# Attention sums in 42 PSUM columns per head, a bf16 state update, and GpSimd left with the mask: a mixed attention and feed-forward kernel

## The chip, the cores and the metric

One NeuronCore of one Trainium2 chip runs the whole program. The metric is the device time of one execution in microseconds (us). The engines are TensorE (PE; its weight loads are listed as PEld), VectorE (DVE), ScalarE (ACT), GpSimd (POOL) and the DMA queue that SyncE issues (SP, in waits SPq). Each engine takes its instructions in the order in which they stand in its program, so an instruction that waits holds up those behind it.

## The reference, cut to what matters

Gated linear attention over 4 batches, 8 heads, 768 steps, head size 40, and then two feed-forward layers over the 3072 tokens (320 to 2048 to 320).

```python
for t in range(S):
    m_new = np.maximum(f_gate[:, :, t] + m, i_gate[:, :, t])
    f_stab, i_stab = np.exp(f_gate[:, :, t] + m - m_new), np.exp(i_gate[:, :, t] - m_new)
    C = f_stab * C + i_stab * outer(v_t, k_t)      # 40 x 40 state per head
    n = f_stab * n + i_stab * k_t
    y[:, :, t] = sigmoid(o_t) * (C @ q_t) / np.maximum(np.abs(n @ q_t), 1.0)
h = np.maximum(x @ w1_in, 0.0);  x = h * h @ w1_out
h = x @ w2_in;  out = h * sigmoid(h) @ w2_out
```

Everything is float32.

## The kernel before, in words

**Attention** runs in 24 tiles of 128 steps of one batch (`TILES`: two batches alternate, six chunks each). In a tile the products within the chunk are matmuls, and a state per batch (`cc2`, 40 rows by 42 columns per head: 40 values, the sum n, a zero) carries over what came before. Tiles 0 to 5 (`N_NAT`) use plain float32 matmuls, the 18 others split float32 numbers into pieces that TensorE multiplies faster. The steps of a tile are functions: `load_a` and `load_b` (DMA of q, k, v; of the broadcast gates `W` and `eq`), `SK`/`SK2` (split q and k on ACT and DVE, then nine small DMAs that restack them, L282 and L284), `WT` (causal mask on POOL L290, exponentials on ACT L294), `SC` (scores, L309, and on DVE their split into three bf16 pieces p1, p2, p3, L316 to L323), `VK` (pieces of v and k, mostly POOL), `QT` (scaled q), `HG` (per head the products p times v and q times state, L400 to L415), `EV` (division and output gate, DVE L426 to L438), `ST` (state update, L476 to L494), `XT` (transpose of the result, L500, to the input x of the feed-forward layers).

In `HG` a head owns 84 PSUM columns, two halves of 42: one matmul of a p piece streams two pieces of v side by side, so four matmuls per head do, and a head group needs two PSUM tiles, hA and hB. `EV` then adds the halves with two TENSOR_REDUCE (L426). `ST` does the same with float32r pieces: six matmuls (khi and klo against vs), two PSUM tiles, two reduces (L478). All these tiles, the scores and the transposes share one PSUM pool of three buffers (tag `at`): seven of them go by per tile of attention.

**Feed-forward layer 1** runs beside attention in 8 blocks of 384 tokens, 16 steps j each: `emit_in` (eight matmuls into `hin`, L569; ACT takes Relu L576 and Square L577; for even j ACT squares again, L579, for odd j DVE does, L581 (`G_PAT = "ad"`); DVE then forms `gl`, L588) and `emit_out` (eight matmuls into `o`). Layer 2 follows alone, 8 blocks more, and is not touched.

**What sets the order.** TensorE's order is written by hand: a table `plan(i)` gives each function of tile i a due time in steps j, relative to `base(i)`; tiles stand 16/3 steps apart. On the other engines a scheduler orders the instructions by its own estimate. During blocks 1 to 6, every sixth step loads one of layer 2's 16 weight pieces, decodes it on ACT, DVE and POOL (`w_split`, L169 to L200) and stores it (L202), all called at one step.

Two small tables choose engines: `ENG` sends `vr`, `vlo`, `kw`, `klo`, `qt`, `ql`, `um`, `clo` and the low parts of weights to POOL.

Of the kernel before, what the change touches and what calls it, by code (L numbers as in the profile page):

```python
# [31 lines left out]
N_NAT = 6  # L32
# [5 lines left out]
G_PAT = "ad"  # L38
# [21 lines left out]
def mlstm_moe_kernel(  # L60
# [104 lines left out]
    def w_split(raw, which, layer, u, pl):  # L165
# [7 lines left out]
        if which == "i":  # L173
# [8 lines left out]
            on("lo_i").tensor_tensor(out=w[:, 3:5], in0=tv[:, 0:2], in1=f(w[:, 0:2]), op=ALU.subtract)  # L182
            on("lo_r").tensor_tensor(out=w[64:128, 2], in0=tv[64:128, 2], in1=f(w[64:128, 2]), op=ALU.subtract)
        else:
# [15 lines left out]
            on("lo_o").tensor_tensor(out=ol, in0=tv, in1=f(oh), op=ALU.subtract)  # L200
        if layer == 2:
            sp.dma_start(out=w2_d[which, u], in_=f(ws))  # L202
# [47 lines left out]
    def load_b(i):  # L250
# [4 lines left out]
        sp.dma_start(out=w, in_=g_d[b * H:(b + 1) * H, c * L:(c + 1) * L].unsqueeze(0).to_broadcast([128, H, L]))  # L255
        if c % EC == 0 and c + EC > 1:
            for g in range(3):
# [3 lines left out]
                             in_=e_d[h:h + n, c * L:(c + EC) * L].unsqueeze(1).to_broadcast([n, 40, EC * L]))  # L261

# [62 lines left out]
    def VK(i):  # L325
# [31 lines left out]
    def QT(i):  # L357
# [6 lines left out]
        on("qt", i).tensor_tensor(out=q, in0=q, in1=eqv(i)[0:120], op=ALU.mult)  # L364
# [3 lines left out]
        on("ql", i).tensor_tensor(out=ql[0:120], in0=q, in1=f(qh[0:120]), op=ALU.subtract)  # L368

    def HG(i, g):  # L370
# [20 lines left out]
        if g == 2:  # L391
            d["hB"] = p_at.tile([128, 512], F32, tag="at", name="hB")
        ps = d["hA"] if g < 2 else d["hB"]
        ov = ps[:, 0:504].rearrange("p (h a c) -> p h a c", a=2, c=42)
        o0 = 3 * (g % 2)
        st = True
        if c:
            k = 40 * n
            cs = cs2[b % 2][0:k, 3 * g:3 * g + n]
            pe.matmul(ov[:, o0:o0 + n], d["qh"][0:k, g], cs, start=True, stop=False)  # L400
            pe.matmul(ov[:, o0:o0 + n, 0], d["ql"][0:k, g], cs[:, :, 0], start=False, stop=False)
            st = False
        for x in (range(n) if HORD else range(n - 1, -1, -1)):
            h = 3 * g + x
            p1, p2, p3 = (d[p, h // 4][:, (h % 4) * L:(h % 4 + 1) * L] for p in ("p1", "p2", "p3"))
            v12, v3 = d["v12"][:, h], d["v3"][:, h]
            o = ov[:, o0 + x]
            if st:
                pe.matmul(o, p2, v12, start=True, stop=False)
                pe.matmul(o[:, 0], p3, v12[:, 0], start=False, stop=False)  # L410
            else:
                pe.matmul(o[:, 0], p3, v12[:, 0], start=False, stop=False)
                pe.matmul(o, p2, v12, start=False, stop=False)
            pe.matmul(o[:, 1], p1, v3, start=False, stop=False)
            pe.matmul(o, p1, v12, start=False, stop=st or x == (n - 1 if HORD else 0))  # L415

    def EV(i):
        d = T[i]
        den = at.tile([128, H, 1], F32, tag="den", name="den")
        if i < N_NAT:  # L420
            hn = d["hA"][:, 0:VW].rearrange("p (h c) -> p h c", c=42)
            act.activation(out=den, in_=hn[:, :, 40:41], func=ACTF.Abs)
        else:
            hn = at.tile([128, H, 42], F32, tag="hn", name="hn")
            for ps, h0, n in ((d["hA"], 0, 6), (d["hB"], 6, 2)):
# [411 lines left out]
```

## Time and profile before

| | |
|---|---|
| median of 3 runs | 932.18 us (930.99 to 933.9) |
| the profiled execution: own time, span | 925.65 us, 923.9 us |
| TensorE busy, granted clock over the span | 844.3 us (91%), 0.987 |
| DVE, ACT, POOL busy | 572.0 us (62%), 497.6 us (54%), 255.8 us (28%) |

The span has two parts. Up to about 578 us attention and layer 1 run together, and every engine works; behind it layer 2 runs alone on a TensorE that is busy in every slice. "Busy" of TensorE is an upper bound, since matmuls overlap in the pipe and their ends are modelled; starts of successive matmuls tell the real rate.

### The profile page before, as it was taken

What the parts mean: (1) busy time and instruction counts of PE and PEld (TensorE: products, weight loads), DVE (VectorE), ACT (ScalarE), POOL (GpSimd) and SP (SyncE); (2) the same over time, 40 slices, a digit from 0 to 9 for tenths busy, and PEclk for the clock granted to TensorE, in tenths of its full rate; (3) what the DMA queues carried; (4) which work ended last, traced back from release to release, by engine and by line L of the source; (5) the groups of instructions that cost most, each with busy time, mean ns of one, the idle gap of its engine ahead of it and who ended that gap; (6) DMA issues with size and microseconds to landing.
All of it is one profiled execution on the core that took longest, in us unless ns stands there. A gap on an engine that the chain in (4) does not pass through costs nothing.

```text
span 923.9 us, 14980 instructions
## 1 busy us (share of the span) xinstructions
PE 844.3 (91%) x5460; PEld 821.4 (89%) x5460; DVE 572.0 (62%) x953; ACT 497.6 (54%) x1061; POOL 255.8 (28%) x271
## 2 busy tenths in 40 slices
PE   3868979889898988988899999999999999999998
PEld 3758969789788988887788999999999999999998
DVE  5567557976888987987987534444445444444343
ACT  3677556665676766665664555343434343444343
POOL 6675344642344555555522010000000000000000
PEclk9999999999999998999999999999999999999999
DMA  8793345555756546545634387110101010000000
GB/s 245 243 299 126 123 150 161 191 153 176 250 176 220 163 140 226 192 140 195 224 123 147 107 309 239 49 57 1 56 1 56 1 57 1 23 1 22 1 22 22
DMA packets 72579, 117.45 MB, mean 127 GB/s; under 512 B 5306, under 2 KB 54394, under 8 KB 72266
## 3 DMA queue, kind: packets, MB, share of 16 engines
q1 hardware_dynamic: 72506, 116.50, 39.1%
q8 instruction: 43, 0.70, 0.3%
q14 instruction: 30, 0.25, 0.1%
HBM read 77.23 MB, written 19.33 MB: 105 GB/s over the span
## 4 chain that ended last, share of the span: by engine, by line
PE 55%; DMA 13%; DVE 12%; ACT 8%; SPq 6%; issue 3%; POOL 2%; ACTq 0%; POOLq 0%; DVEq 0%
PE hin L569 27%; PE o L621 6%; PE o L619 6%; PE o L620 6%; SPq L284 3%; DMA vk<-in_vk_dram 3%; ACT W L294 2%; DMA eq<-e_d 2%; DMA stk<-tt 2%; DMA raw<-in_w_in_dram 2%; PE o L602 2%; DVE gl L588 2%; PE o L603 2%; PE o L604 2%; SPq L282 1%
## 5 line engine op out<-in xcount | busy, mean ns | idle before, releaser
L569 PE MATMUL hin<-x,wi 128*128 128x384 f32 x2048 | 416.7, 345 | 23.6 <-ACT r L576 10.5
L569 PEld LDWEIGHTS hin<-x,wi 128*128 128x128 f32 x2048 | 364.6, 192 | 29.7 <-ACT r L576 12.9
L588 DVE TENSOR_TENSOR gl<-r,gh 128x384 fp32r<-128x384 f32 x256 | 163.6, 642 | 92.0 <-ACT gh L585 68.2
L584 DVE TENSOR_TENSOR r<-hin,r 128x384 f32<-128x384 f32 x128 | 71.3, 557 | 122.1 <-ACT r L583 122.1
L583 ACT ACTIVATE r<-hin 128x384 f32<-128x384 f32 x128 | 63.0, 492 | 132.4 <-PE hin L569 132.4
L621 PE MATMUL o<-wo,gl 128*128 128x320 f32 x384 | 118.7, 309 | 0.0
L619 PE MATMUL o<-wo,gh 128*128 128x320 f32 x384 | 118.3, 308 | 0.0
L620 PE MATMUL o<-wo,gh 128*128 128x320 f32 x384 | 117.8, 307 | 0.0
L585 ACT ACTIVATE gh<-r 128x384 fp32r<-128x384 f32 x128 | 67.2, 525 | 74.0 <-DVE r L584 74.0
L602 PE MATMUL o<-gh,wo 128*128 128x384 f32 x256 | 90.5, 353 | 4.3 <-ACT ob L612 3.8
L576 ACT ACTIVATE r<-hin 128x384 f32<-128x384 f32 x128 | 61.4, 480 | 57.8 <-PE hin L569 39.2
L604 PE MATMUL o<-gl,wo 128*128 128x384 f32 x256 | 86.8, 339 | 1.4 <-DVE gl L588 1.4
L603 PE MATMUL o<-gh,wo 128*128 128x384 f32 x256 | 86.8, 339 | 0.0
L619 PEld LDWEIGHTS o<-wo,gh 128*128 128x128 f32 x384 | 72.1, 188 | 0.0
L620 PEld LDWEIGHTS o<-wo,gh 128*128 128x128 f32 x384 | 72.1, 188 | 0.0
L621 PEld LDWEIGHTS o<-wo,gl 128*128 128x128 f32 x384 | 72.0, 187 | 0.0
L647 POOL TENSOR_TENSOR xr<-xr 128x384 f32<-128x384 f32 x8 | 8.1, 1017 | 230.0 <-DMA xr<-x_d 179.7
L294 ACT ACTIVATE W<-W,aw 128x128 f32<-128x128 f32 x192 | 60.2, 389 | 17.0 <-POOL W L290 16.9
L577 ACT ACTIVATE gh<-r 128x384 fp32r<-128x384 f32 x128 | 66.5, 521 | 2.2
L581 DVE TENSOR_TENSOR r<-r 128x384 f32<-128x384 f32 x64 | 47.1, 737 | 21.5 <-ACT gh L577 21.5
L602 PEld LDWEIGHTS o<-gh,wo 128*128 128x128 f32 x256 | 49.0, 191 | 5.6 <-ACT ob L612 4.5
L604 PEld LDWEIGHTS o<-gl,wo 128*128 128x128 f32 x256 | 48.7, 190 | 2.0 <-DVE gl L588 2.0
(147 smaller groups left out, 1365.7 us busy)
## 6 DMA issues: line engine op xcount, KB each, us to landing
stk<-tt SPq DMA_DIRECT2D x162, 120.0 KB
raw<-in_w_in_dram SPq DMA_DIRECT2D x16, 768.0 KB
W<-g_d SPq DMA_DIRECT2D x24, 512.0 KB
raw<-in_w_out_dram SPq DMA_DIRECT2D x16, 640.0 KB
vk<-in_vk_dram SPq DMA_DIRECT2D x24, 328.0 KB
rqk<-in_qk_dram SPq DMA_DIRECT2D x18, 360.0 KB
w2i_d<-ws SPq DMA_DIRECT2D x8, 640.0 KB
w2o_d<-ws SPq DMA_DIRECT2D x8, 640.0 KB
```

Source lines behind the costliest of these rows:

```text
L294: act.activation(out=w[:, h], in_=w[:, h], func=ACTF.Exp, bias=aw[:, 0, c, r0 + h:r0 + h + 1])
L569: pe.matmul(ps[:, 0:N], w[:, c, ws], x[:, sl, 0:N], start=(k == 0), stop=(k == 7))
L577: act.activation(out=gh, in_=r, func=ACTF.Square)
L584: dve.tensor_tensor(out=g, in0=ps[:, 0:N], in1=r, op=ALU.mult)
L585: act.activation(out=gh, in_=g, func=ACTF.Copy)
L588: low.append(lambda: on("gl" if ly == 1 else "gl2", gi).tensor_tensor(out=gl, in0=g, in1=f(gh), op=ALU.subtract))
L602: pe.matmul(o[k][:, 0:N], w[:, c], gh, start=first, stop=False)
L603: pe.matmul(o[k][:, 0:N], w[:, c2], gh, start=False, stop=False)
L604: pe.matmul(o[k][:, 0:N], w[:, c], gl, start=False, stop=last)
L619: pe.matmul(o[k][:, 0:DM], gh[:, c], w[:, 0:320], start=first, stop=False)
L620: pe.matmul(o[k][:, 0:DM], gh[:, c], w[:, 320:640], start=False, stop=False)
L621: pe.matmul(o[k][:, 0:DM], gl[:, c], w[:, 0:320], start=False, stop=last)
```

## The change

- **HG and EV:** a head owns 42 columns, one PSUM tile holds all eight heads. Six matmuls per head (`PAIRS`: piece of p, piece of v) add up in them, and three float32r matmuls per group instead of two. No reduce: `EV` reads PSUM directly, the absolute value becomes two small DVE operations, the copy of 64 columns goes from ACT to DVE.
- **ST:** three bf16 pieces each of k and v (`d["k"]`, `d["v"]`), 18 bf16 matmuls into one PSUM tile, no reduce; the state grows straight from PSUM. For the first chunk ACT copies it.
- **POOL to DVE:** behind tile 5 all of `VK`, `QT`, the state's mask and split, and the low parts of layer 2's weights are on DVE; POOL keeps the causal mask.
- **DVE to ACT:** `G_PAT = "a"`, ACT squares for every j. `r` has three buffers instead of two.
- **Due times:** `load_b` is split in `load_w` and `load_e`; layer 2's weights are loaded, decoded and stored at separate due times (17, 19 and 21.5 steps, one piece every 6).

```diff
+PAIRS = ((2, 0), (1, 0), (1, 1), (0, 2), (0, 1), (0, 0))
-G_PAT = "ad"
+G_PAT = "a"
...
-            on("lo_i").tensor_tensor(out=w[:, 3:5], in0=tv[:, 0:2], in1=f(w[:, 0:2]), op=ALU.subtract)
+            eng = pool if layer == 1 else dve
+            eng.tensor_tensor(out=w[:, 3:5], in0=tv[:, 0:2], in1=f(w[:, 0:2]), op=ALU.subtract)
...
         if layer == 2:
-            sp.dma_start(out=w2_d[which, u], in_=f(ws))
+            raws["st", which, u] = lambda: sp.dma_start(out=w2_d[which, u], in_=f(ws))
...
-        on("vr", i).tensor_tensor(out=r, in0=v, in1=top(v), op=ALU.subtract)
+        dve.tensor_tensor(out=r, in0=v, in1=top(v), op=ALU.subtract)
...
+        d["v"] = [x.rearrange("p (h c) -> p h c", c=42) for x in (top(v), top(r), v3)]
         if c < NC - 1:
-            act.activation(out=vs[:, :, 0], in_=v0, func=ACTF.Copy)
-            on("vlo", i).tensor_tensor(out=vs[:, :, 1], in0=v0, in1=f(vs[:, :, 0]), op=ALU.subtract)
-            on("kw", i).tensor_tensor(out=k0, in0=k0, in1=wv, op=ALU.mult)
-            act.activation(out=khi[:, 0:DM], in_=k, func=ACTF.Copy)
-            on("klo", i).tensor_tensor(out=klo[:, 0:DM], in0=k, in1=f(khi[:, 0:DM]), op=ALU.subtract)
+            dve.tensor_tensor(out=k0, in0=k0, in1=wv, op=ALU.mult)
+            kr = at.tile([128, DM], F32, tag="kr", name="kr")
+            dve.tensor_tensor(out=kr, in0=k, in1=top(k), op=ALU.subtract)
+            k3 = at.tile([128, DM], BF16, tag="k3", name="k3")
+            dve.tensor_tensor(out=k3, in0=kr, in1=top(kr), op=ALU.subtract)
+            d["k"] = [top(k), top(kr), k3]
...
-            pe.matmul(ov[:, o0:o0 + n], d["qh"][0:k, g], cs, start=True, stop=False)
-            pe.matmul(ov[:, o0:o0 + n, 0], d["ql"][0:k, g], cs[:, :, 0], start=False, stop=False)
+            pe.matmul(o, d["qh"][0:k, g], cs[:, :, 0], start=True, stop=False)
+            pe.matmul(o, d["qh"][0:k, g], cs[:, :, 1], start=False, stop=False)
+            pe.matmul(o, d["ql"][0:k, g], cs[:, :, 0], start=False, stop=False)
...
+            for m, (x, y) in enumerate(PAIRS):
+                pe.matmul(ov[:, h], ps[x], d["v"][y][:, h], start=c == 0 and m == 0, stop=m == len(PAIRS) - 1 and (c == 0 or h == 3 * g + n - 1))
...
-                dve.tensor_reduce(out=hn[:, h0:h0 + n],
+        dve.tensor_scalar(out=den, in0=hn[:, :, 40:41], scalar1=-1.0, scalar2=1.0, op0=ALU.mult, op1=ALU.max)
+        dve.tensor_tensor(out=den, in0=den, in1=hn[:, :, 40:41], op=ALU.max)
...
-                    pe.matmul(o, khi[:, ks], vs[:, h:h + n], start=True, stop=False)
-                    pe.matmul(o[:, :, 0], klo[:, ks], vs[:, h:h + n, 0], start=False, stop=True)
-                dve.tensor_reduce(out=u[0:120, h0:h1],
+            for m, (x, y) in enumerate(pairs):
+                pe.matmul(ps[0:40 * n, h:h + n], ks[x][:, 40 * h:40 * h + 40 * n], vp[y][:, h:h + n],
+                          start=m == 0, stop=m == len(pairs) - 1)
...
-        r = mp.tile([128, NMAX], F32, tag="r", name="r")[:, 0:N]
+        r = mp.tile([128, NMAX], F32, tag="r", name="r", bufs=3)[:, 0:N]
...
+            for at_, fn in ((17.0, lambda e=e: w_load(2, e, stp)), (19.0, lambda e=e: w_dec(2, e, stp)),
+                            (21.5, lambda e=e: raws.pop(("st", *e))())):
+                events.setdefault(int(2 * (at_ + 6 * k)), []).append((at_ + 6 * k, fn))
...
-                    if ly == 1 and 0 < n <= 6 and (16 * n + j) % 6 == 3:
-                        e = wq[(16 * (n - 1) + j) // 6]
-                        w_load(2, e, stp)
-                        w_dec(2, e, stp)
```

DVE at the end of one tile in the middle of the first part (gl and r: layer 1; hn, den, y: `EV`; st, u, cc: `ST`), before:

```order
L280 TENSOR_TENSOR tt<-rqk,tt 120x2x384
L426 TENSOR_REDUCE hn<-hA 128x252
L426 TENSOR_REDUCE hn<-hB 128x84
L429 SCALAR_TENSOR_TENSOR den<-hn 128x8
L437 TENSOR_TENSOR y<-hn,sg 128x320
L431 TENSOR_SCALAR den<-den 128x8
L432 RECIPROCAL den<-den 128x8
L438 TENSOR_TENSOR y<-y,den 128x320
L581 TENSOR_TENSOR r<-r 128x384
L337 TENSOR_TENSOR v_3880<-vk 128x336
L588 TENSOR_TENSOR gl<-r,gh 128x384
L478 TENSOR_REDUCE u<-st 120x252
```

and the same place of the change:

```order
L284 TENSOR_TENSOR tt<-rqk,tt 120x2x384
L407 TENSOR_SCALAR den<-hA 128x8
L367 TENSOR_TENSOR ql<-rqk,qh 120x384
L408 TENSOR_TENSOR den<-den,hA 128x8
L414 TENSOR_TENSOR y<-hA,sg 128x320
L409 RECIPROCAL den<-den 128x8
L415 TENSOR_TENSOR y<-y,den 128x320
L416 COPY y<-y 128x64
L549 TENSOR_TENSOR gl<-r,gh 128x384
L346 TENSOR_TENSOR kr<-vk 128x320
L427 SCALAR_TENSOR_TENSOR cc_115<-cc_115,eq_111,st 120x126 x2
L427 SCALAR_TENSOR_TENSOR cc_115<-cc_115,eq_111,st 80x84
```

The reduces and layer 1's square are gone; `ql` and `kr` now stand among the steps of `EV` and `ST`.

POOL over one tile in the middle of the first part (ql, rqk: `QT`; vk, klo, vs: `VK`; u, cs: `ST`), before:

```order
L335 TENSOR_TENSOR vk<-vk 128x336
L344 TENSOR_TENSOR vk<-vk,aw 128x320
L290 AFFINE_SELECT W<-W 128x512 x2
L346 TENSOR_TENSOR klo<-vk,khi 128x320
L492 TENSOR_TENSOR u<-cc_118,bmask 120x336
L343 TENSOR_TENSOR vs<-vk,vs 128x8x42
L364 TENSOR_TENSOR rqk<-rqk,eq_114 120x384
L494 TENSOR_TENSOR cs_116<-u,cs_116 120x8x42
L368 TENSOR_TENSOR ql<-rqk,qh 120x384
```

and of the change, from the last of layer 1's weights to layer 2:

```order
L198 TENSOR_TENSOR wo_1215<-dt,wo_1215 128x2x64
L450 TENSOR_TENSOR cm<-cc_116,bmask 120x336
L337 TENSOR_TENSOR vk<-vk,aw 128x320
L363 TENSOR_TENSOR q<-q,eq_112 120x384
L294 AFFINE_SELECT W<-W 128x512 x34
L608 TENSOR_TENSOR xr<-xr 128x384 x8
```

Of nine instructions per tile two masks are left.

SP where a weight piece of layer 2 is stored (w2i_d), among the DMAs that restack q and k (stk), before:

```order
L162 DMA raw<-in_w_out_dram 128x1280
L282 DMA stk<-tt 40x2x384
L284 DMA stk<-tt 40x768
L202 DMA w2i_d<-ws 128x1280
L284 DMA stk<-tt 40x768
L282 DMA stk<-tt 40x2x384
```

and of the change:

```order
L236 DMA rqk<-in_qk_dram 120x768
L163 DMA raw<-in_w_out_dram 128x1280
L204 DMA w2i_d<-ws 128x1280
L286 DMA stk<-tt 40x2x384
L288 DMA stk<-tt 40x768 x2
```

The store stands ahead of the nine DMAs and no longer between them.

## Rows read from the trace of the kernel before

**Rows 1.** Windows by block: us, PE, PEld, DVE, ACT, POOL busy, PEclk, DMA

```profile
77.70:152.50 74.80, 67.27 (x446) 64.01 (x445) 52.27 (x89) 43.56 (x102) 34.53 (x37) 0.98 0.41 127
152.50:481.20 328.70, 291.45 (x2083) 278.46 (x2082) 275.02 (x454) 217.18 (x486) 155.35 (x153) 0.97 0.57 184
481.20:533.40 52.20, 50.01 (x348) 49.20 (x347) 32.47 (x55) 26.26 (x53) 7.90 (x7) 1.00 0.43 143
533.40:578.00 44.60, 44.60 (x258) 43.97 (x258) 18.10 (x31) 23.29 (x44) 2.93 (x3) 1.00 0.82 273
```

**Rows 2.** Timeline of TensorE, one tile's HG, ST, SC, XT: start, us, line

```profile
306.64 0.28 PE L400 MATMUL hA<-cs,qh 120*128 120x252 f32 x1
306.76 0.22 PE L401 MATMUL hA<-cs,ql 120*128 120x126 f32 x1
306.82 0.20 PE L412 MATMUL hA<-vk,p 128*128 128x42 bf16 x1
...
307.23 0.36 PE L400 MATMUL hA<-cs,qh 120*128 120x252 f32 x1
...
308.39 1.65 PE L569 MATMUL hin<-x,wi 128*128 128x384 f32 x8
...
312.66 0.28 PE L476 MATMUL st<-vs,khi 128*120 128x252 f32 x1
...
313.24 0.42 PE L602 MATMUL o<-gh,wo 128*128 128x384 f32 x1
...
316.13 0.56 PE L309 MATMUL sc<-stk 120*128 120x128 f32 x4
316.53 0.39 PE L602 MATMUL o<-gh,wo 128*128 128x384 f32 x1
...
319.83 0.49 PE L500 MATMUL xT<-ident,y 128*128 128x128 f32 x3
320.07 0.42 PE L602 MATMUL o<-gh,wo 128*128 128x384 f32 x1
```

**Rows 3.** Waits of TensorE, 152.5 to 481.2 us: total, times, longest

```profile
PE hin L569 <- ACT r L576: 6.9, 5, 2.9
PE xT L500 <- DVE y L438: 6.9, 4, 2.7
PE st L476 <- DVE hn L426: 5.6, 4, 3.6
PE sc L309 <- DVE u L478: 5.1, 5, 1.5
PE hin L569 <- DVE x L507: 3.6, 3, 1.2
PE hin L569 <- ACT x L506: 2.8, 2, 1.8
```

**Rows 4.** Groups of DVE, 152.5 to 481.2 us: busy, mean ns, idle before

```profile
L588 DVE TENSOR_TENSOR gl<-r,gh 128x384 fp32r<-128x384 f32 x81 | 57.5, 715 | 7.6 <-ACT r L579 6.7
L581 DVE TENSOR_TENSOR r<-r 128x384 f32<-128x384 f32 x40 | 31.6, 790 | 2.6 <-ACT gh L577 2.6
L280 DVE TENSOR_TENSOR tt<-rqk,tt 120x768 fp32r<-120x768 f32 x15 | 14.4, 959 | 33.3 <-ACT tt L270 33.3
L426 DVE TENSOR_REDUCE hn<-hA 128x252 f32<-128x504 f32 x15 | 10.1, 676 | 0.0
```

**Rows 5.** Windows of L588 alone, 600 to 900 us: us, DVE busy

```profile
600.00:900.00 300.00, 62.31 (x110) 1.00 0.07 23
```

**Rows 6.** Chain that ended last, 246 to 256 us: start, us, what

```profile
247.17 5.58 DMA raw<-in_w_in_dram
...
253.56 0.49 ACT r L576
```

**Rows 7.** Waits of POOL, 152.5 to 481.2 us: total, times, longest

```profile
POOL vk L335 <- DMA vk<-in_vk_dram: 21.5, 8, 7.1
...
POOL rqk L364 <- DMA eq<-e_d: 16.2, 10, 2.6
```

More of the change, by code (lines that the diff above doesn't have):

```diff
@@ L390, in HG @@
             d["hA"] = p_at.tile([128, 512], F32, tag="at", name="hA")
[L391 to L396, printed above, removed]
+        ov = d["hA"][:, 0:VW].rearrange("p (h c) -> p h c", c=42)
         if c:
@@ L399, in HG @@
             cs = cs2[b % 2][0:k, 3 * g:3 * g + n]
-            pe.matmul(ov[:, o0:o0 + n], d["qh"][0:k, g], cs, start=True, stop=False)
-            pe.matmul(ov[:, o0:o0 + n, 0], d["ql"][0:k, g], cs[:, :, 0], start=False, stop=False)
[L402 to L415, printed above, removed]
+            o = ov[:, 3 * g:3 * g + n]
+            pe.matmul(o, d["qh"][0:k, g], cs[:, :, 0], start=True, stop=False)
+            pe.matmul(o, d["qh"][0:k, g], cs[:, :, 1], start=False, stop=False)
+            pe.matmul(o, d["ql"][0:k, g], cs[:, :, 0], start=False, stop=False)
+        for h in range(3 * g, 3 * g + n):
+            ps = [d[x, h // 4][:, (h % 4) * L:(h % 4 + 1) * L] for x in ("p1", "p2", "p3")]
+            for m, (x, y) in enumerate(PAIRS):
+                pe.matmul(ov[:, h], ps[x], d["v"][y][:, h], start=c == 0 and m == 0, stop=m == len(PAIRS) - 1 and (c == 0 or h == 3 * g + n - 1))
     def EV(i):
@@ L419, in EV @@
         den = at.tile([128, H, 1], F32, tag="den", name="den")
[L420 to L425, printed above, removed]
-                dve.tensor_reduce(out=hn[:, h0:h0 + n],
-                                  in_=ps[:, 0:84 * n].rearrange("p (h a c) -> p h c a", a=2, c=42),
-                                  axis=AXL.X, op=ALU.add)
-            dve.scalar_tensor_tensor(out=den, in0=hn[:, :, 40:41], scalar=-1.0, in1=hn[:, :, 40:41],
-                                     op0=ALU.mult, op1=ALU.max)
-        dve.tensor_scalar(out=den, in0=den, scalar1=1.0, scalar2=None, op0=ALU.max)
+        hn = d["hA"][:, 0:VW].rearrange("p (h c) -> p h c", c=42)
+        dve.tensor_scalar(out=den, in0=hn[:, :, 40:41], scalar1=-1.0, scalar2=1.0, op0=ALU.mult, op1=ALU.max)
+        dve.tensor_tensor(out=den, in0=den, in1=hn[:, :, 40:41], op=ALU.max)
         dve.reciprocal(out=den, in_=den)
@@ L438, in EV @@
         on("y2", i).tensor_tensor(out=yv, in0=yv, in1=den.to_broadcast([128, H, D]), op=ALU.mult)
[L439 removed]
+        dve.tensor_copy(out=y[:, 320:384], in_=y[:, 256:320])
     def ST(i):
@@ L451, in grow @@
                                      scalar=eqv(i)[0:m, h0 // 3, L - 1:L], in1=src, op0=ALU.mult, op1=ALU.add)
+        ps = p_at.tile([128, 512], F32, tag="at", name="st")[:, 0:VW].rearrange("p (h c) -> p h c", c=42)
         if i < N_NAT:
-            ps = p_at.tile([128, 512], F32, tag="at", name="st")[:, 0:VW].rearrange("p (h c) -> p h c", c=42)
             vkt = T[i]["vk"]
-            v = vkt[:, DM:DM + VW].rearrange("p (h c) -> p h c", c=42)
+            ks, vp, pairs = [vkt], [vkt[:, DM:DM + VW].rearrange("p (h c) -> p h c", c=42)], ((0, 0),)
+        else:
+            ks, vp, pairs = T[i]["k"], T[i]["v"], PAIRS
@@ L457, in ST @@
+        for h in (0, 3, 6):
+            n = min(3, H - h)
+            for m, (x, y) in enumerate(pairs):
+                pe.matmul(ps[0:40 * n, h:h + n], ks[x][:, 40 * h:40 * h + 40 * n], vp[y][:, h:h + n],
+                          start=m == 0, stop=m == len(pairs) - 1)
+        if c == 0:
+            act.activation(out=cv[:, 0:6], in_=ps[0:120, 0:6], func=ACTF.Copy)
+            act.activation(out=cv[0:80, 6:8], in_=ps[0:80, 6:8], func=ACTF.Copy)
+        else:
             for h in (0, 3, 6):
```

78 lines of the change are left out of this document (24 added, 54 removed).

## The prediction

> **What bounds the kernel now.** I read the windows by block first [rows 1]. The last block of layer 1 runs without attention and takes 44.6 us with TensorE busy throughout: that is layer 1's floor. The five blocks from 152.5 to 481.2 us take 328.7 us, 65.7 each, with three tiles of attention in each. In them no engine is full: TensorE is idle for 328.7 - 291.45 = 37.3 us, DVE is busy for 275.0 us (84%), ACT for 217.2 us, POOL for 155.4 us.
>
> Next, the timeline of TensorE gives the floor of a tile [rows 2], by starts: HG from 306.64 to 308.39, 1.75 us; ST from 312.66 to 313.24, 0.58; one half of SC from 316.13 to 316.53, 0.40, so 0.80 for both; XT from 319.83 to 320.07, 0.24. Together 3.37 us. Three tiles and the 44.6 make 54.7 us per block, 273.6 for five. The blocks stand 55.1 us above this floor. Of that 37.3 us is idle; the other 17.8 us TensorE counts as busy but runs behind the floor, with a mean granted clock of 0.97 in these windows against 1.00 in the last block [rows 1].
>
> Then the waits of TensorE in these blocks [rows 3] say what is late. 5.6 and 5.1 us are ST and SC waiting for a PSUM buffer that a reduce of `EV` or `ST` still reads. 6.9 us are XT waiting for `y`, the end of `EV`. 3.6 and 2.8 us are the first matmul of a block waiting for `x`, which is made from XT. 6.9 us are `hin` waiting for ACT. One of these is in the chain: ACT stands at the decoding of a weight piece whose DMA was issued at 247.17 and landed 5.58 us later, and `r` of layer 1, queued behind it, comes at 253.56 [rows 6].
>
> Last, DVE [rows 4]. `gl` takes 715 ns here and 62.31 / 110 = 566 ns in layer 2, where POOL hardly works [rows 5]: beside a busy POOL, DVE's work is slower.
>
> **The change, part by part.**
>
> *HG on TensorE.* Per head 6 matmuls in place of 4, 16 pairs of load and matmul more per tile. Twelve pairs take 307.23 - 306.82 = 0.41 us, 34 ns each [rows 2], over matmuls of 42 and 84 columns in turn. If a pair's price goes with its columns, 48 pairs of 42 cost what 32 of 63 on average cost, nothing more; if it goes with the load, 16 x 34 = 0.54 us more. I take 0.35. The float32r part streams 3 x 126 columns in place of 252 + 126, no more columns, but loads weights once more per group. Lower bound 0; upper bound a load that shows in full, 0.40 / 4 = 100 ns as in SC [rows 2], 0.3 per tile. I take 0.2. In all 0.55 us for each of 18 tiles, 10 us (0 to 15).
>
> *ST on TensorE.* 18 bf16 pairs in place of 6 float32r matmuls, in the 14 split tiles whose chunk is not the last. If a pair costs 34 ns as in HG, 18 make 0.61 us, nothing new. If it costs what a float32r matmul of ST costs, 0.58 / 6 = 97 ns, they make 1.75 us, 1.17 more. The operands are like HG's, but the stationary one has 120 or 80 columns and not 128; I take the middle, 0.075 us: 0.77 more per tile, 11 us (0 to 16). The Trainium skill, "TensorE: Matmul & The Clock Gate", sections "LDWEIGHTS (loading the stationary operand)" and "Weight-path perf modes — Fast Weight Load (FWL) and DoubleRow", speaks against this step: the fast load needs exactly 128 columns, and without it a load takes the columns divided by 1.2 ns. By that an estimate for ST is 12 x 100 + 6 x 67 = 1600 ns, 1.02 us more and 14 us for 14 tiles, which would put the sum 3 us higher; no row here shows a bf16 load of 120 columns.
>
> TensorE pays 21 us (0 to 31), nothing hides it where TensorE is the bound.
>
> *PSUM.* Five buffers of tag `at` per tile in place of seven. The waits on reduces, 5.6 + 5.1 = 10.7 us [rows 3], should go. What is late next there is the state's growth, which now reads PSUM itself.
>
> *EV.* Two reduces (676 ns the larger [rows 4]) leave the way from HG to XT, and so does the step through ACT for the copy. The waits for `y` and `x`, 6.9 + 3.6 + 2.8 = 13.3 us [rows 3], I expect to shrink by two thirds, 8.9 us.
>
> *ACT and the weights.* ACT takes 40 squares more in these blocks (as long as the other squares, some 0.5 us, the length of `r` at 253.56 [rows 6]: 20 us) and loses three copies per tile (15 x 3 x 0.5, 22 us): even, at 66%. The weights are due two steps, some 5.5 us at 44.6 / 16 per step, ahead of their decoding, about the 5.58 us that ACT stood behind one [rows 6]; with the third `r` buffer I take two thirds off the 6.9 us for ACT, 4.6 us. The store of a piece no longer stands on SP between the DMAs that restack q and k.
>
> *DVE.* In the five blocks it loses 31.6 us of squares and four reduces per tile: 676 ns for 504 elements [rows 4], by elements 1.8 us for the tile's 1344, 27 us. It gains eight operations per tile of 320 to 384 elements at no more than 566 ns [rows 5], 15 x 8 x 0.566 = 68 us, and the low parts of 13 weight pieces, about 1 us each by their 640 to 768 elements, 13 us. With POOL down to two masks per tile the slowing goes: 81 x (715 - 566) = 12 us on `gl` alone [rows 4, 5], and if the rest of its work with two inputs in SBUF, about as much again, gains in proportion, 30 us in all. 275 - 32 - 27 + 81 - 30 = 267 us: as full as before, no relief and no new bound. I count nothing for it.
>
> **The sum.** In the five blocks the waits shrink by 10.7 + 8.9 + 4.6 = 24.2 us of 37.3. The 17.8 us behind the floor go with them in proportion, 11.6 us. The block from 77.7 us, with only one split tile, I credit 1 us; the one from 481.2 us, 52.2 us long and at its floor, gains nothing. So -24.2 - 11.6 - 1 + 21 = -15.8 us. The profiled execution took 925.65 us itself, and becomes 909.8. The median of the runs is 932.18, 6.5 us more; I forecast 909.8 + 6.5 = **916 us**. Layer 2 after 578 us stays as it is.
>
> **The rivals.**
>
> *All these waits go, TensorE pays little.* The 30.9 us of rows 3 go, 14.8 of the 17.8 with them, and TensorE pays half my price, 10 us: -36.7, 896 us. For it: the block from 481.2 us, where DVE is only 62% busy, runs at its floor. Against it: DVE stays as full as in the five blocks.
>
> *The waits only change their names.* DVE and ACT are as full as before, so only the 10.7 us on PSUM buffers and 5.1 behind them go: -15.8 - 1 + 21 = +4, about 936 us, and with a TensorE price a little under mine 932. For it: nothing in the sum relieves DVE.
>
> *DVE stands in its queue, and it gets slower.* `vr` and `kw` wait for the DMA of vk, `qt` for that of eq, `ql` for ACT. On POOL these DMAs cost 21.5 + 16.2 = 37.7 us of waiting [rows 7], where nobody was behind them in a hurry. On DVE each such wait holds `gl` of layer 1 and the scores' pieces behind it. DVE's work of 267 us, its own wait for `tt`, 33.3 us [rows 4], and all 37.7 us make 338 us, 9.3 more than the five blocks take now; with TensorE's 3 us in the other blocks 925.65 + 12.3 + 6.5 = 944 us. It decides from 328.7 - 267 - 33.3 = 28 us of moved waits on. Against it: POOL was idle half of the time and met these DMAs early; DVE comes to them later.
>
> That the change does not do what it says is excluded by the order: 34 masks in a row on POOL, no reduce on DVE.
>
> **How the numbers follow.** Forecast 0.52 (903 to 928 by the bounds of TensorE's price and a third more or less of the waits), the first rival 0.20, the second 0.15, the third 0.13. What a measurement of this kernel tells from no change is 0.3%, 929.4 to 935.0 us. Faster: 0.52 + 0.20 + a third of the second, 0.05, 0.77. Same: 0.08. Slower: 0.02 + 0.13 = 0.15. The range leaves out half of the first rival and most of the third: 894 to 938 us.
>
> **What would show it.** Right: no wait of ST or SC on DVE's reduces; blocks of some 62 us; the pairs of ST 60 to 100 ns apart; POOL near 5 us per block; `gl` near 0.6 us; ACT's wait for the landing of a weight gone. Wrong: DVE idle behind DMA vk or eq for more than 28 us (third rival), or waits of TensorE for `y`, `gl` and p in the place of those on PSUM (second). The forecast falls altogether if the part after 578 us changes, or if blocks come out shorter than 58 us or longer than 65.7.

## The result and the profile after

The change takes 918.5 us (median of 4 runs, 916.17 to 919.5) against 931.59 us before: a ratio of 0.9864, 95% interval 0.9818 to 0.9909. Faster, by some 13 us (1.4%). The profiled execution took 918.51 us itself (span 916.8 us), its median; the one of before, 925.65 us, had been 6 us under its own. The two profiles therefore differ by 7.1 us only.

Engines of the whole span, page of the changed kernel:

```profile
PE 860.2 (94%) x5964; PEld 839.9 (92%) x5964; DVE 513.4 (56%) x1001; ACT 515.5 (56%) x1071; POOL 94.6 (10%) x121
```

Windows, the five blocks with three tiles each (153.6 to 474.0 us), changed kernel: busy time and instructions of PE, PEld, DVE, ACT, POOL, granted clock, DMA share, GB/s:

```profile
153.60:474.00 320.40, 301.82 (x2519) 292.36 (x2517) 231.79 (x496) 225.67 (x489) 22.37 (x30) 0.97 0.60 190
```

They took 328.7 us before [rows 1], so they carry the profiles' difference (-8.3 us). TensorE is idle for 18.6 us where it was for 37.3, and busy 10.4 us longer. VectorE has **more** instructions (496 for 454) and is busy 43 us **less**. The clock is the same 0.97.

Waits of TensorE there, changed kernel: total, times, longest in us:

```profile
PE hA L401 <- DVE p L327: 8.9, 6, 2.3
PE hin L530 <- ACT r L537: 4.5, 4, 2.9
PE o L563 <- ACT ob L573: 3.5, 1, 3.5
PE o L565 <- DVE gl L549: 1.3, 1, 1.3
PE hin L530 <- DVE x L468: 0.4, 1, 0.4
```

The waits on PSUM reduces and on `y` [rows 3] are gone. The largest is now that of the head product for the third piece of the scores, which was small in the same blocks before:

```profile
PE hA L412 <- DVE p L323: 1.8, 2, 1.2
```

VectorE's groups there by shape, changed kernel: count, busy us, mean ns, idle before:

```profile
L549 DVE TENSOR_TENSOR gl<-r,gh 128x384 fp32r<-128x384 f32 x80 | 44.3, 557 | 12.8 <-ACT r L540 12.7
L326 DVE TENSOR_TENSOR pr<-W 128x512 f32<-128x512 f32 x30 | 20.9, 698 | 0.0
L327 DVE TENSOR_TENSOR p<-pr 128x512 bf16<-128x512 f32 x30 | 20.6, 685 | 0.0
L320 DVE TENSOR_TENSOR W<-sc,W 128x512 f32<-128x512 f32 x30 | 20.5, 684 | 2.4 <-PE sc L313 2.3
```

`gl` takes 557 ns where it took 715 [rows 4]. How that comes about is the main find of the runs.

### The profile page after: what moved, and what is told of

It reads as the page before. It is cut to its first block, busy times and chain, and to the rows that moved or that the text cites. A ratio compares the mean times of both kernels' runs of the same rounds, so it can differ in the third digit from the quotient of the medians.

```text
span 916.8 us, 15812 instructions
## 1 busy us (share of the span) xinstructions
PE 860.2 (94%) x5964; PEld 839.9 (92%) x5964; DVE 513.4 (56%) x1001; ACT 515.5 (56%) x1071; POOL 94.6 (10%) x121
## 4 chain that ended last, share of the span: by engine, by line
PE 62%; DMA 15%; ACT 8%; DVE 7%; SPq 4%; issue 2%; POOL 1%; POOLq 0%; ACTq 0%; DVEq 0%
PE hin L530 29%; DMA W<-g_d 8%; PE o L582 6%; PE o L580 6%; PE o L581 6%; ACT W L298 3%; DMA eq<-e_d 3%; PE o L563 2%; PE o L565 2%; PE o L564 2%; SPq L288 2%; PE hA L401 2%; DVE gl L549 1%; DMA stk<-tt 1%; PE o L568 1%
## 5 line engine op out<-in xcount | busy, mean ns | idle before, releaser
L549 DVE TENSOR_TENSOR gl<-r,gh 128x384 fp32r<-128x384 f32 x256 | 147.3, 577 | 131.1 <-ACT gh L546 68.9
L563 PE MATMUL o<-gh,wo 128*128 128x384 f32 x256 | 91.8, 359 | 3.9 <-ACT ob L573 3.9
L564 PE MATMUL o<-gh,wo 128*128 128x384 f32 x256 | 87.6, 342 | 0.0
L294 POOL TENSOR_SCALAR_AFFINE_SELECT W<-W 128x512 f32<-128x512 f32 x48 | 35.7, 768 | 346.8 <-DMA W<-g_d 129.9
L540 ACT ACTIVATE r<-r 128x384 f32<-128x384 f32 x128 | 66.8, 522 | 2.6
```

Of the source, the lines that this page charges most:

```text
L549: low.append(lambda: on("gl" if ly == 1 else "gl2", gi).tensor_tensor(out=gl, in0=g, in1=f(gh), op=ALU.subtract))
L563: pe.matmul(o[k][:, 0:N], w[:, c], gh, start=first, stop=False)
L564: pe.matmul(o[k][:, 0:N], w[:, c2], gh, start=False, stop=False)
```

## The experiments

Each kernel was run beside the kernel before on the same chip; a ratio is to that, with its 95% interval. "Blocks" are the five blocks of the profiled execution (from the windows by block; those of before start 0.1 us later here than in [rows 1]), then TensorE's and VectorE's busy time in them.

| kernel | median us | ratio | blocks | PE | DVE (instr.) | clock |
|---|---|---|---|---|---|---|
| before | 930.06 to 930.88 | 1 | 328.6 | 291.4 | 274.9 (454) | 0.97 |
| change again | 918.59 | 0.9871 [0.9829, 0.9914] | 323.3 | 303.5 | 232.1 (495) | 0.96 |
| change, GpSimd's work back | 928.33 | 0.9966 [0.9939, 0.9994] | 326.9 | 302.5 | 221.8 (385) | 0.97 |
| change, half the squares on VectorE | 921.39 | 0.9903 [0.9872, 0.9934] | 330.6 | 305.8 | 252.4 (533) | 0.95 |
| change, head product as before | 918.19 | 0.9862 [0.9821, 0.9903] | 318.2 | 293.7 | 249.0 (525) | 0.98 |
| change, due times as before | 920.82 | 0.9880 [0.9837, 0.9924] | 319.9 | 304.2 | 231.5 (492) | 0.96 |
| change, state update as before | 921.37 | 0.9889 [0.9838, 0.9940] | 319.3 | 298.6 | 245.8 (524) | 0.97 |
| change, both products as before | 923.02 | 0.9916 [0.9887, 0.9945] | 327.0 | 290.2 | 257.6 (553) | 0.96 |
| change, head product later | 933.48 | 1.0038 [1.0014, 1.0063] | 336.1 | 303.2 | 233.6 (494) | 0.96 |
| before, new due times | 931.20 | 1.0003 [0.9968, 1.0038] | 331.3 | 295.3 | 275.9 (455) | 0.96 |
| before, GpSimd's work on VectorE | 929.79 | 0.9985 [0.9954, 1.0016] | 334.1 | 296.1 | 270.8 (576) | 0.95 |
| the same, squares on ScalarE | **912.56** | 0.9807 [0.9781, 0.9833] | 317.4 | 288.4 | 255.0 (537) | 0.98 |
| the same, 42 columns per head | 926.48 | 0.9946 [0.9923, 0.9969] | 330.3 | 305.1 | 246.2 (522) | 0.94 |

**The change once more** (unchanged).

> The changed kernel once more, as the mark for the runs beside it and to see how far one kernel's profiled executions differ. Theory W (the gain is the PSUM, y and x waits that go, less a dearer head product, and part of it is lost again to the new wait of the head product on the third p piece): 916 to 920 us, blocks 1 to 5 at 320 us, TensorE's wait of hA on VectorE's p at 6 to 11 us there. If the stretches at the granted clock of 0.5 are chance and not set by the kernel, this execution puts them at other places and their sum moves by more than 7 us from the 34 us of the execution seen so far; if they are set by the waits, they lie at the same tiles.

918.59 us. TensorE's waits are nearly the same (p 9.5 us in 6, `r` 5.3 in 4), and four of the stretches with a granted clock near 0.5 lie at the same places in both (132 to 140, 180 to 188, 372 to 380, 436 to 444 us). Others don't: from 60 to 480 us they sum up to 27 us here and 34 there. They set in around the end of TensorE's longest waits, with some chance: in the first execution a stretch follows the wait of 3.46 us that begins at 217.2 and none the one of 2.93 at 244.6; here one follows that of 4.04 at 239.7 and none that of 3.30 at 213.8.

**GpSimd gets its work back.**

```diff
-        dve.tensor_tensor(out=r, in0=v, in1=top(v), op=ALU.subtract)
+        pool.tensor_tensor(out=r, in0=v, in1=top(v), op=ALU.subtract)
...
-        dve.tensor_tensor(out=ql[0:120], in0=q, in1=f(qh[0:120]), op=ALU.subtract)
+        pool.tensor_tensor(out=ql[0:120], in0=q, in1=f(qh[0:120]), op=ALU.subtract)
```

(so too the products and pieces of k, q and the state, and the weights' low parts.)

> The changed kernel with the eleven elementwise operations per tile (values, keys, queries, state mask and split) and the low parts of layer 2's weights given back to GpSimd; PSUM columns, pieces and due times stay. Theory W: these operations are off the chain, and VectorE's queue gets shorter in front of the p pieces, so the wait of hA on p shrinks from 8.9 to about 4 us, and GpSimd is late for a few of them: 914 to 922 us. Theory U (the gain comes of GpSimd being idle, which lets VectorE's operations run shorter: gl 557 ns against 715 before): gl goes back to about 700 ns, VectorE's 232 us of blocks 1 to 5 lose less than the 35 us moved, and the time returns to 928 to 934 us.

928.33 us: of the 12 us of gain, 9.7 are gone, as theory U said. VectorE loses 111 instructions and only 10 us. The timelines of GpSimd and of VectorE in this kernel show why (start, us, engine, line):

```profile
198.79 1.32 POOL L363 TENSOR_TENSOR rqk<-rqk,eq 120x384 f32<-120x384 f32 x1
208.66 1.01 POOL L367 TENSOR_TENSOR ql<-rqk,qh 120x384 fp32r<-120x384 f32 x1 [8.55 <-ACT qh L366]
```

```profile
199.16 1.50 DVE L326 TENSOR_TENSOR pr<-W 128x512 f32<-128x512 f32 x1
200.59 0.68 DVE L320 TENSOR_TENSOR W<-sc,W 128x512 f32<-128x512 f32 x1
...
202.25 0.68 DVE L326 TENSOR_TENSOR pr<-W 128x512 f32<-128x512 f32 x1
...
209.04 1.06 DVE L549 TENSOR_TENSOR gl<-r,gh 128x384 fp32r<-128x384 f32 x1 [0.44 <-ACT r L540]
```

The `pr` that starts at 199.16, while GpSimd is at work until 200.11, ends 0.55 us behind that end; the one at 202.25, with GpSimd idle, takes 0.68. `gl` at 209.04 ends 0.43 us behind GpSimd's `ql`. VectorE does not run slower, it stands until GpSimd is done. The timelines of both engines over the five blocks say the same for all: of the 30 `pr`, 15 take 1.2 us or more, and each of them ends 0.55 us behind a GpSimd instruction that had begun before it; three that began before a GpSimd TENSOR_TENSOR take under 0.7. Of the 80 `gl`, 23 are lengthened, and each ends some 0.4 us behind one. One line's durations over 153 to 475 us (min/median/max ns), `pr` and then the product of scores and weights, in this kernel:

```profile
L326 DVE TENSOR_TENSOR pr<-W x29: 674/692/1775, 154.8 to 463.4; 128x512 f32<-128x512 f32 x29
```

```profile
L320 DVE TENSOR_TENSOR W<-sc,W x29: 675/678/692, 153.5 to 461.8; 128x512 f32<-128x512 f32 x29
```

Both have the same shape. `pr` reads two operands in SBUF and takes up to 1775 ns; L320 reads one of its two in PSUM and never exceeds 692, beside the same GpSimd: six of them began while one of its TENSOR_TENSOR ran. The Trainium skill, "SBUF — State Buffer", section "Who interferes with whom", says the same: a VectorE instruction with two inputs in SBUF contends with a GpSimd instruction that reads SBUF, and the later one blocks until the first ends; with one SBUF input, outside its 2-port modes, it does not. These rows agree with it in both halves. The mask that GpSimd keeps does the same, rarely: one `pr` of the changed kernel takes 1114 ns behind one.

How much of the 9.7 us comes of these stalls is not parted from GpSimd's own lateness: in this kernel VectorE also waits 16.6 us for its `vk` and 4.5 us for its `kr`.

**Squares back on VectorE**, in part.

```diff
-G_PAT = "a"
+G_PAT = "ad"
```

> The changed kernel with every second square of the first stage computed by VectorE again instead of ScalarE (one word of a pattern). Theory W: VectorE gets 40 operations of about 0.65 us in blocks 1 to 5, some 26 us, and ScalarE loses 40 of about 0.5; the wait of hA on p grows by a third to a half (8.9 to about 13 us) and little else moves: 920 to 926 us. Theory S (the squares are where the gain is, since r on VectorE was a wait of its own): the wait of hin on r of VectorE comes back with 3 to 6 us and the time goes to 927 to 933 us.

921.39 us, in theory W's range: 2.8 us more, with intervals that overlap. The squares alone are not the place of the gain. But the wait on p, which W let grow, shrank to 2.8 us; those on `gl` (8.9), ACT's `r` (8.3) and `x` (4.2) came in its place.

**The head product and its eviction as before.**

```diff
-        ov = d["hA"][:, 0:VW].rearrange("p (h c) -> p h c", c=42)
+        if g == 2:
+            d["hB"] = p_at.tile([128, 512], F32, tag="at", name="hB")
+        ps = d["hA"] if g < 2 else d["hB"]
+        ov = ps[:, 0:504].rearrange("p (h a c) -> p h a c", a=2, c=42)
...
+                dve.tensor_reduce(out=hn[:, h0:h0 + n],
```

> The changed kernel with the head product and the eviction alone as before: 84 columns per head in two PSUM tiles, two reduces on VectorE, nothing else changed. TensorE gets back 18 to 19 tiles of 0.68 us, some 13 us. Theory W: the three attention PSUM buffers are short again, the waits of st and of sc on the reduces come back with 6 to 10 us in blocks 1 to 5, and the two reduces (1.9 us per tile) stand in VectorE's queue before the next p pieces: 918 to 928 us, no faster than the change. Rival P (the 42 columns cost more than they bring, the gain is from the rest of the change): 904 to 912 us.

918.19 us, the change's own time: the 42 columns, which give the change its name, come out even here. TensorE is busy 8 us less in the five blocks and idle 6 us more. Waits of TensorE in this kernel, 153 to 475 us:

```profile
PE hA L413 <- DVE p L327: 8.7, 7, 2.4
PE xT L485 <- DVE y L440: 4.5, 4, 3.0
PE hin L554 <- DVE x L492: 4.1, 3, 3.2
PE hin L554 <- ACT r L561: 3.4, 4, 2.1
```

`y` and `x` come late again, 9.9 us of waits in all (1.3 of it for `y` of L439) where the change has 0.4: what the shorter eviction brings, the dearer product takes. But no matmul waits for the reduces, with one PSUM tile per tile of attention more than the change, and my expectation of 6 to 10 us there fell. Since the state's two reduces are missing here, this alone does not tell a late VectorE from a lack of buffers; the kernels below with all seven PSUM tiles do in part.

**The due times as before** (in `plan`, and the weights loaded, decoded and stored at one step).

```diff
-        for k, e in enumerate(wq):
-            for at_, fn in ((17.0, lambda e=e: w_load(2, e, stp)), (19.0, lambda e=e: w_dec(2, e, stp)),
-                            (21.5, lambda e=e: raws.pop(("st", *e))())):
...
+                    if ly == 1 and 0 < n <= 6 and (16 * n + j) % 6 == 3:
```

> The changed kernel with the due times of before (loads, key and value splits, eviction, and layer 2's weights loaded, decoded and stored at one step). After the first runs theory U leads (idle GpSimd lets VectorE's operations run shorter: 98% of the change's gain went when GpSimd got the operations back, with the same due times). Theory U: the times are worth 0 to 4 us, 918 to 923. Theory D (the due times carry the gain, since they keep loads and weight decoding out of the way): 926 to 932 us.

920.82 us, intervals overlapping with the change's: theory U. (GpSimd's work had taken 9.7 of 12.2 us back, 80% of the gain and not the 98% of the expectation.)

**The state update as before.**

```diff
-            d["k"] = [top(k), top(kr), k3]
+            act.activation(out=khi[:, 0:DM], in_=k, func=ACTF.Copy)
+            dve.tensor_tensor(out=klo[:, 0:DM], in0=k, in1=f(khi[:, 0:DM]), op=ALU.subtract)
...
+                dve.tensor_reduce(out=u[0:120, h0:h1],
```

> The changed kernel with the state update as before: float32r pieces, 84 columns, two PSUM tiles and two reduces, its splits on VectorE. TensorE gets back some 13 times 0.34 us, 4 us; VectorE gets two reduces of 0.67 and 0.32 us per tile and loses the bf16 third pieces of the keys, ScalarE two copies per tile. Theory U (PSUM columns and pieces are a small matter either way): 915 to 922 us. Theory W (the shorter state update is part of the gain): 923 to 928 us, with waits of xT or sc on the reduces.

921.37 us (914.03 to 926.76): within theory U's range, too wide for a sign.

**The kernel before with the new due times alone** (the edit of the due times, reversed, in the kernel before).

> The kernel before with the due times of the change and nothing else (84 columns, float32r state, GpSimd's work, squares on both engines as before). Theory U: within 4 us of before, 926 to 932 us, VectorE's gl still at about 715 ns. Theory D: most of the gain is here, 917 to 923 us.

931.20 us, 1.0003 of before, `gl` at 735 ns. The due times are not the gain either.

**The kernel before with GpSimd's work on VectorE alone.**

```diff
-        on("vr", i).tensor_tensor(out=r, in0=v, in1=top(v), op=ALU.subtract)
+        dve.tensor_tensor(out=r, in0=v, in1=top(v), op=ALU.subtract)
...
-            on("klo", i).tensor_tensor(out=klo[:, 0:DM], in0=k, in1=f(khi[:, 0:DM]), op=ALU.subtract)
+            dve.tensor_tensor(out=klo[:, 0:DM], in0=k, in1=f(khi[:, 0:DM]), op=ALU.subtract)
```

> The kernel before with GpSimd's elementwise operations of the tiles after the first ones and the low parts of layer 2's weights on VectorE, and nothing else (84 columns, reduces, float32r state, half the squares on VectorE, due times as before). Theory U: gl falls from 715 to about 560 ns and the p pieces from 858 and 892 to about 690, so that VectorE's busy time in blocks 1 to 5 grows by 25 us at most although it gets some 110 instructions more (0.5 us each alone are 55 us): 918 to 926 us. Theory W (the gain is the waits on PSUM tiles and y, which this kernel keeps, behind a longer VectorE queue): 931 to 940 us.

929.79 us, between the two ranges: theory U was right about VectorE's durations and wrong about the time; of theory W the waits came, the longer time did not. Windows of this kernel's five blocks, then one line's durations:

```profile
153.00:487.10 334.10, 296.07 (x2082) 284.65 (x2082) 270.78 (x576) 215.49 (x482) 26.61 (x30) 0.95 0.57 182
```

```profile
L322 DVE TENSOR_TENSOR pr<-W x29: 678/683/692, 155.0 to 469.1; 128x512 f32<-128x512 f32 x29
```

VectorE does 122 instructions more in 4 us less, and no `pr` takes over 692 ns. Yet nothing is won: the queue stays as full, and `y` comes late, for which TensorE waited 6.9 us before [rows 3]. Waits of TensorE:

```profile
PE xT L500 <- DVE y L438: 17.5, 6, 6.2
PE xT L500 <- ACT y L439: 13.3, 8, 3.0
PE st L476 <- DVE hn L426: 3.2, 3, 2.6
```

So it seems that GpSimd's idleness must meet room in VectorE's queue. That is theory Q of the runs that follow.

**The same, with all squares on ScalarE** (`G_PAT = "a"` in that kernel).

> The kernel before with GpSimd's operations on VectorE, and now also all squares of the first stage on ScalarE; columns, reduces, float32r state and due times of before. With the operations alone moved, VectorE's were short (gl 558 ns) but xT waited 30.8 us for y. Theory Q (the gain needs both: GpSimd idle, so that VectorE's operations are short, and room in VectorE's queue, so that y and the reduces are not late): 31 us of squares leave VectorE in blocks 1 to 5, xT's waits for y fall to 5 to 15 us, and the time is 919 to 926 us. Rival C (only the short chain of the 42 columns, without reduces, gets y out in time): xT's waits for y stay over 20 us, 927 to 934 us.

**912.56 us**, 17.2 less than without the squares and 6 less than the change; the interval of its ratio (to 0.9833) ends just about where that of the change's second set (from 0.9829) begins. Windows and waits of TensorE in this kernel's five blocks:

```profile
151.30:468.70 317.40, 288.36 (x2083) 276.56 (x2082) 254.99 (x537) 235.31 (x524) 25.01 (x30) 0.98 0.59 190
```

```profile
PE xT L500 <- DVE y L438: 9.9, 4, 5.3
PE xT L500 <- ACT y L439: 9.6, 6, 4.5
PE hin L569 <- DVE x L507: 2.2, 3, 0.9
```

The waits for `y` fell from 30.8 to 19.5 us, less than theory Q asked (5 to 15) and just under rival C's 20; the time decides against C, and lies 6 us under theory Q's range too. Two moves between engines, without columns, pieces, due times or buffers, beat the whole change. The squares alone, with GpSimd's work where it was, were not tried in this kernel, so that both moves are needed is shown for one of them only. Against the squares alone speaks the change with GpSimd's work back: it has all squares on ScalarE, beside the new products, and won 2.4 us.

**The change with both products as before** (the edits of the head product and of the state update together).

> The changed kernel with both products as before: 84 columns and two reduces in the head product and its eviction, float32r pieces, two PSUM tiles and two reduces in the state update. Engines, squares, due times and the three buffers of r are those of the change. Each of the two alone cost nothing (918.2 and 921.4 us against 918.6). Theory Q (columns and pieces are a trade that comes out even): 916 to 923 us. Rival C (either of them is enough to keep PSUM tiles free, so that each alone hid the other's worth): waits on PSUM reduces of 10 us and more, 925 to 932 us.

923.02 us, at the end of Q's range, with 22.3 us of waits for `y`. With all seven PSUM tiles per tile of attention, waits on reduces are back, though half of rival C's 10 us:

```profile
PE sc L318 <- DVE u L484: 3.1, 4, 1.3
PE st L482 <- DVE hn L432: 2.0, 2, 1.4
```

They were 10.7 us before [rows 3] and are 2.7 in the fastest kernel, which has seven tiles too. So most of them had been VectorE's lateness, and the number of tiles has a part. Without either product the change loses 4.4 us, with intervals that just overlap: in a queue that holds all reduces, the short eviction may be worth something. This kernel differs from the fastest one by the due times, the three buffers of `r`, the copy of `y` on VectorE and the place of v's third piece, and is 10.5 us slower. Which of them costs that was not tried.

**The head product half a step later.**

```diff
-                    (b + 3.2, lambda: (HG(i, 0), HG(i, 1), HG(i, 2))), (b + 3.9, lambda: EV(i)),
+                    (b + 3.7, lambda: (HG(i, 0), HG(i, 1), HG(i, 2))), (b + 4.4, lambda: EV(i)),
```

> The changed kernel with the head products due half a step later, and eviction, state update, the load of the decay row after it and the transposes 0.4 to 0.5 later with it. Theory Q (the last wait that costs time is that of the head product on the third p piece, and y now has room to spare): the wait falls from 9 us to under 3, those of xT and hin on y and x stay under 3, and with the waits some of the stretches at the granted clock of 0.5 go: 907 to 914 us. Rival V (VectorE's bursts are a step longer than that and only move: p is late at other tiles, or x comes late for the next block): 916 to 924 us.

933.48 us, slower than both expectations. The wait on p is gone, and larger ones stand for it (waits of TensorE in this kernel's five blocks):

```profile
PE hin L530 <- ACT r L537: 17.0, 7, 3.8
PE hin L530 <- ACT x L467: 6.7, 2, 3.5
PE hin L530 <- DVE x L468: 5.4, 3, 2.5
```

The last tile of a block now makes `x` late for the next one; why `r` costs 17.0 us here stays open. There was no room behind the head product; the 9 us on p are cheaper than what removes them.

**The fastest kernel with the 42 columns.**

> The kernel before with GpSimd's operations on VectorE and all squares on ScalarE (912.6 us), and now the head product in 42 columns and its shorter eviction from the change as well; state update and due times of before. It prices the change's head product where VectorE has room. Theory Q (the columns are a trade that comes out even or worse: TensorE's busy time in blocks 1 to 5 grows by 15 times 0.68, some 10 us, and the 19.5 us of xT's waits for y fall, but these were partly room that the dearer product now fills): 910 to 918 us, with xT's waits for y under 8 us. Theory C (the short chain of the columns is a gain of its own once the queue has room): 900 to 908 us. Theory P (the dearer product is paid in full since the waits only change place, to the third p piece): 918 to 924 us.

926.48 us: 13.9 more, beyond even theory P. Windows and waits of TensorE in its five blocks:

```profile
154.80:485.10 330.30, 305.11 (x2361) 294.88 (x2360) 246.17 (x522) 234.87 (x510) 23.87 (x30) 0.94 0.57 183
```

```profile
PE hA L404 <- DVE p L324: 7.6, 5, 2.2
PE hin L549 <- ACT r L556: 5.1, 2, 3.9
PE hin L549 <- DVE x L487: 2.9, 3, 1.7
```

The waits for `y` fall to 3.1 us, as wanted, but TensorE's idle time only from 29.0 to 25.2, and its busy time grows by 16.8. Some 7.7 us are the product itself: 15 tiles of 0.51, and not the 0.68 of the expectation (see the head product's price below). The rest goes with the clock of 0.94 for 0.98; how much of the 13.9 us is chance of the clock stays open.

## Why the prediction was right, and where it was not

The forecast of 916 us holds (918.5 measured), in the likeliest case. Most of its terms do not.

**VectorE, counted at nothing, carries most of the gain.** The step "267 us: as full as before, no relief" failed: it is 231.8. The moved work takes 66 us, not 81 (the groups of that work by line), and what else went, some 50 us, was put at 30: 274.9 - 31.6 of squares - 27.8 of reduces + 66.5 - 231.8 = 50. It holds the stalls behind GpSimd, and what the eviction and the state's growth save by reading PSUM. I had read `gl` at 715 against 566 ns [rows 4, 5] rightly, and scaled it with `gl`'s share; `pr` and p, at 858 and 892 ns against 698 and 685, lost more. Before:

```profile
L323 DVE TENSOR_TENSOR p<-pr 128x512 bf16<-128x512 f32 x30 | 26.7, 892 | 0.3
L322 DVE TENSOR_TENSOR pr<-W 128x512 f32<-128x512 f32 x31 | 26.6, 858 | 0.6
```

Giving GpSimd its work back takes 9.7 of the 12 us.

**PSUM: right result, cause only in part.** The 10.7 us on reduces went, as forecast. But they stay away too with one tile more per head product, and with all seven tiles 5.1 or 2.7 us come back once GpSimd's work and the squares have moved: VectorE had been late, more than buffers were short.

**The eviction** was forecast at 8.9 us and brings about that: 9.9 us of waits for `y` and `x` with the head product as before, 0.4 in the change. But it pays for the dearer product and no more: undoing both costs nothing.

**ACT and the weights.** The waits of `hin` for `r` fell by 2.4 us (6.9 to 4.5), not 4.6, and not through the weights: ACT waits longer for their landing than before, 13.5 us (9.4 and 4.1) against 10.5 (4.3, 3.4 and 2.8). What went are the 13.0 us that its `r` waited behind `gl`; the third buffer of `r`, the forecast's other reason, may be why, and was not tried alone.

**The head product's price**: forecast 0.55 us per tile, measured 0.51. Timeline of TensorE, changed kernel, a tile with a wait (first rows, the wait, the instruction behind it) and the next tile, without one (first row, the instruction behind it):

```profile
309.19 0.22 PE L395 MATMUL hA<-cs,qh 120*128 120x126 f32 x1
...
309.48 0.20 PE L401 MATMUL hA<-vk,p 128*128 128x42 bf16 x1
...
309.59 0.21 PE L401 MATMUL hA<-vk,W 128*128 128x42 bf16 x2
309.64 0.18 PE L401 MATMUL hA<-vk,p 128*128 128x42 bf16 x1
...
309.94 0.31 PE L395 MATMUL hA<-cs,qh 120*128 120x126 f32 x1
...
310.43 0.21 PE L401 MATMUL hA<-vk,W 128*128 128x42 bf16 x2
311.38 0.19 PE L401 MATMUL hA<-vk,p 128*128 128x42 bf16 x1 [0.74 <-DVE p L327]
...
312.36 0.42 PE L530 MATMUL hin<-x,wi 128*128 128x384 f32 x1
...
331.58 0.23 PE L395 MATMUL hA<-cs,qh 120*128 120x126 f32 x1
...
333.84 0.42 PE L563 MATMUL o<-gh,wo 128*128 128x384 f32 x1
```

The tile without a wait takes 2.26 us from start to start, against 1.75 [rows 2]: 0.51 more. The other gives the same if the wait is counted by starts: from 309.59 to 309.64 the next one follows 0.05 us later, from 310.43 to 311.38 it is 0.95, so 0.90 of the 3.17 us are the wait. (The 0.74 beside it counts from the modelled end of the matmul before, and to subtract it alone gives 0.68, the price that two of my expectations used.) TensorE's busy time, 8 us less with the head product as before, agrees with 15 x 0.51. Of the parts, 18 pairs from 309.48 to 309.94 are 26 ns each, so a pair did get cheaper with fewer columns: 48 cost some 0.17 us more than the 32 of before, not 0.35. The float32r part is the dearer one: 0.29 us in the first group, from 309.19 to 309.48, where it was 0.18 [rows 2], some 0.33 per tile, not 0.2. Two errors cancel in the 0.55.

**The state update's price**: forecast 0.77, measured 0.34 (316.66 to 317.58, 0.92 us against 0.58). Same view:

```profile
316.66 0.22 PE L439 MATMUL st<-vk,k 128*120 128x126 bf16 x1
...
317.36 0.20 PE L439 MATMUL st<-vk,k 128*80 128x84 bf16 x1
...
317.58 0.42 PE L563 MATMUL o<-gh,wo 128*128 128x384 f32 x1
```

12 pairs with 126 columns in 0.70 us are 58 ns each, 6 with 84 are 37: they go with the moving columns (before, a pair of 84 behind a stationary operand of 128 takes 38 to 40 ns in HG). By the Trainium skill, "TensorE: Matmul & The Clock Gate", sections "LDWEIGHTS (loading the stationary operand)" and "Weight-path perf modes — Fast Weight Load (FWL) and DoubleRow", a load of 120 columns takes 100 ns (estimate from columns divided by 1.2 ns) and has no fast load. That is not the pace here. The records of these loads are indeed longer, 133 to 135 ns on average against 98 to 100 for the 128 columns of HG, but they overlap and start 58 ns apart. The measurement decides, and taking the middle was too dear.

**The sum.** In the five blocks, with 15 head products and 13 split state updates, the floor rose by 15 x 0.51 + 13 x 0.34 = 12.1 us (forecast 18.3, by the same counts), to 285.7, and what stands above it fell from 55.1 to 34.7, 20.4 us (forecast 35.8). The idle part fell from 37.3 to 18.6, 18.7 us: the reduces gave 10.7, `y` and `x` 12.9 (13.3 to 0.4, more than their 8.9), ACT's `r` 2.4, and the wait on p, which stood in no term of the sum, took 7.1 back (1.8 to 8.9).

The largest miss is the part behind the floor. It was to shrink in proportion to the waits, by 11.6 us, and shrank by 1.7 (17.8 to 301.8 - 285.7 = 16.1). That step failed: fewer waits did not bring a better clock, 0.97 in both, with some 17 us of the blocks at the lower of the two clock levels, 1.2 GHz, before and 20 after (windows of 4 us). In all -8.3 came of the blocks where -17.5 was forecast.

That the median is within 2.5 us of the forecast is luck in part. The 6.5 us that I added for the distance of profile and median belonged to that execution of before alone; the changed one is at its median. They hide most of what the profiled execution missed by: 909.8 forecast, 918.5 measured.

**The signs.** Blocks of 64.1 us for 62, POOL at 4.5 us per block for 5 and `gl` at 557 ns for 0.6 us are near; the pairs of ST, 58 and 37 ns apart, lie under the 60 to 100, and ACT's wait for weights did not go.

**The rivals.** That all waits go (896 us) fails on p. That waits only change names (932 to 936) is right in mechanism for p, too small to decide. That VectorE stands in its queue for DMAs: 9.2 us for vk and 5.8 for eq, with 2.3 more for eq in front of `tt` some 17 in all, under the 28 from which it decides. Its cousin came true in the kernel before with only the move (waits for `y` of 30.8 us behind a full queue).

## What to carry to other kernels

Where VectorE and GpSimd both work on SBUF, look at the spread of one VectorE line (minimum, median, maximum): a long tail for lines with two SBUF operands and none for lines that read PSUM means that one engine stands behind the other, and work given to GpSimd then saves VectorE little or nothing (here 10 us of busy time for 111 instructions in the change, less than nothing for 122 in the kernel before). In this kernel such a move paid with room in the queue that receives it: the move alone was worth 1 us, the two together 18; the squares alone were not tried. When a price is read from a tile with a wait in it, take the wait by starts, or take a tile without one. And a change of many parts is worth taking apart even when it wins: the part that names this one came out even in it, and cost 14 us in the best version.

## What was not expected of the hardware

- Work on GpSimd cost VectorE as much time as the work itself would have: 122 instructions moved over made VectorE's busy time 4 us shorter (270.8 us against 274.9).
- bf16 stationary operands of 120 columns follow each other at 58 ns with 126 moving columns, those of 80 at 37 ns with 84, though the records of their loads are 133 and 114 to 117 ns long.
- 7.7 us more work for TensorE (15 head products in 42 columns, in the fastest kernel) went with 16.8 us more busy time: the mean granted clock of the five blocks fell from 0.98 to 0.94, more of it at the 1.2 GHz level. Part of this is the chance of two executions, of which one lies 3.2 us above its kernel's median and the other 1.8 under. The clock of the whole span, 0.971 against 0.989 in these two, is 0.977 against 0.983 in the median of all, and the median times differ by 13.9 us.
